# A decayed-attention, top-2 experts and feed-forward kernel on one core: one tile's routing in runs on VectorE, TensorE's fillers in a PSUM bank of their own, changed costs and due times in the scheduler, router constants loaded first

## The chip, the cores and the metric

The kernel runs on one core of one Trainium2 chip. The metric is device time in microseconds (us), the median over timed runs; lower is better. Five engines work side by side, each through its own list of instructions in order: TensorE (PE; its weight loads are shown as PEld), VectorE (DVE), ScalarE (ACT), GpSimd (POOL) and SyncE (SP, which only issues DMA transfers). An instruction waits on semaphores that other engines or transfers raise. SBUF is the on-chip memory that all of them read and write; PSUM is the one that TensorE writes to, in banks of 128 x 512 float32.

## The reference

Three layers follow each other, for 3072 tokens of 384 numbers.

```python
# 1. attention: 4 batches, 8 heads, 768 steps, 48 numbers per head
for t in range(S):
    state = alpha[:, :, t, :, None] * state + np.einsum('bhd,bhe->bhde', k[:, :, t], v[:, :, t])
    y[:, :, t] = np.einsum('bhd,bhde->bhe', q[:, :, t], state)
x = y.transpose(0, 2, 1, 3).reshape(B * S, H * D)          # 3072 x 384
# 2. eight experts, two of them for each token
logits = x @ w_gate
noisy = logits + np.log1p(np.exp(x @ w_noise)) * noise
top2 = indices of the two largest of 8;  top2_w = softmax over the two
h = np.maximum(x[mask] @ w1[e], 0.0)                       # 384 -> 1024
out[mask] += top2_w[mask, k, None] * (h @ w2[e])           # 1024 -> 384
# 3. last layer
h = x @ w_in                                               # 384 -> 2048
return np.maximum(0.01 * h, h) @ w_out                     # 2048 -> 384
```

## The kernel before

**Attention.** The 3072 tokens are 24 units of 128 tokens; four units form a tile, so there are six tiles (0 to 5). SyncE loads three tiles per unit: `at` (the decays, 112x517 float32), `kq` (keys and queries, 112x1024) and `nv` (values, 128x512). ScalarE takes a sum of squares of `at` (L959). VectorE then does the same list for each unit: a backward scan `suf` over 512 columns (L965), twice a reciprocal of two columns and a forward scan `wt` over 256 (L973, L974), the scaled keys `kt` (L988) and the scaled queries `qp` (L992). TensorE transposes the keys, multiplies scores `pS`/`pT` (L1013), updates the state `pM` (L1048, L1052) and sums `pY` (L1069, L1076). GpSimd applies the causal masks to the scores (L1022) and the decay to the state (L1039). The last step of a unit on TensorE is `turn_y` (L1098): four matmuls transpose y into the bank `pA` and multiply it by the router's weights, which stand beside the identity in `turn_w`. ScalarE copies the transposed rows out (into a tile named `xg`), VectorE reduces the logits `lg` (L1107).

**Fillers.** Where the scheduler sees a gap on TensorE it puts in matmuls with the identity whose results nobody reads (`keep_busy`, L919). They write into the last 128 columns of the PSUM tile `pC`. The first columns of that same tile are the operands `d1f`, `d1b`, `scb` of the three scans: `pC` is written by L973 and read by L965 and L974.

**Routing of a tile.** When its four logits are there, a chain of some 30 small operations, called links, runs: `gate_top2` (L204 on, mostly 128x32 on VectorE, three on ScalarE) yields noisy logits `g_z`, the maxima `g_m` and the one-hot choices `g_oh`; three more links count the choices (L1145 to L1153); TensorE and ScalarE make positions out of the counts (L1162, into `pA`); and three links (L1174, L1180, L1184) yield `si`, the slot of each row in the buffer `x_s` in DRAM. GpSimd then scatters the tile's rows into their slots by eight indirect DMAs (L1191), two for each unit.

**Experts and last layer.** Each expert's rows lie in `x_s` in groups: the rows of the first four tiles for experts 0 and 1 (`EARLY`, `EARLY_TILES`), which are worked on first, then the other groups. A group's rows are loaded (L526, tile `xg`), three transposed blocks of 128 go through `pA` (L600), ScalarE rounds them to `xh`, and VectorE subtracts, to `xl` (L609). Expert weights come in four blocks per expert, each a `w1s` (128x768) and a `w2s` (128x768), and are split in the same way into a rounded part (ScalarE, L464) and a rest (`split_lo`, L468, on VectorE or GpSimd, whichever the scheduler finds earlier). TensorE then forms each product in three passes (hi x hi, lo x hi, hi x lo): `ph` (L742) and `py` (L781). The last layer takes the sums of each token's two experts and runs through the same loops.

**The order.** A class `Planner` writes all instruction lists before the kernel runs. Every step has an engine (or a choice "vg" of VectorE and GpSimd), an assumed duration, predecessors, rings of buffers that it takes and holds, and a due time, which is the earliest of those of its successors less their durations, and of a time given by hand. The planner steps through an assumed clock: it takes the step that can start first on any engine, and among several ready ones the one due first. The phase of attention is 1, that of the experts 2. The ring `pA` has two buffers (`ps2`, a pool of two PSUM banks); `turn_y`, the positions and the row transpositions take turns in it. Dependencies between transfers and reads are found by the framework; `apart` removes those among scatters and loads that touch different slots, so that a load of first rows waits for the scatters of tiles 0 to 3 and not for later ones.

## Time and profile before

| | |
|---|---|
| median of 3 timed runs | 1096.68 us (1092.26 to 1100.07) |
| the profiled execution | 1087.71 us |
| its span, first to last instruction | 1085.9 us |
| granted TensorE clock, mean | 0.983 of full speed |
| TensorE busy | 1042.8 us (96%) |
| VectorE busy | 593.7 us (55%) |
| ScalarE busy | 388.2 us (36%) |
| GpSimd busy | 278.5 us (26%) |

Busy time is a mean over stages that differ. In the strip of 40 slices of the span (27.1 us each) TensorE shows 6 tenths in the first slice, 8 in the fifth, 5 in the seventh (163 to 190 us), 7 in the last and 9 or more in all others; the granted clock is lowest in the seventh, with 7 tenths. All durations in the rows below come from the one profiled execution, which lies 9.0 us below the median of the timed runs.

### The profile page before, as it was taken

What the parts mean: (1) busy time and instruction counts of PE and PEld (TensorE: products, weight loads), DVE (VectorE), ACT (ScalarE), POOL (GpSimd) and SP (SyncE); (2) the same over time, 40 slices, a digit from 0 to 9 for tenths busy, and PEclk for the clock granted to TensorE, in tenths of its full rate; (3) what the DMA queues carried; (4) which work ended last, traced back from release to release, by engine and by line L of the source; (5) the groups of instructions that cost most, each with busy time, mean ns of one, the idle gap of its engine ahead of it and who ended that gap; (6) DMA issues with size and microseconds to landing.
All of it is one profiled execution on the core that took longest, in us unless ns stands there. A gap on an engine that the chain in (4) does not pass through costs nothing.

```text
span 1085.9 us, 18172 instructions
## 1 busy us (share of the span) xinstructions
PE 1042.8 (96%) x6839; PEld 999.2 (92%) x6839; DVE 593.7 (55%) x1218; ACT 388.2 (36%) x825; POOL 278.5 (26%) x321
## 2 busy tenths in 40 slices
PE   6999895999999999999999999999999999999997
PEld 5887775999999999999999989899999999999997
DVE  5998997223464565646574233455554545454543
ACT  3755644223354544445453222222222222212211
POOL 3466876200032253424351021410110100000000
PEclk9998997999999999999999999999999999999999
DMA  9667746413464565746567344320101100000000
GB/s 232 203 203 242 237 129 222 157 50 103 148 201 141 179 200 164 226 142 207 180 222 241 116 153 139 92 66 9 59 22 45 34 33 16 22 1 23 1 22 26
DMA packets 78917, 133.20 MB, mean 123 GB/s; under 512 B 8514, under 2 KB 56260, under 8 KB 78820
## 3 DMA queue, kind: packets, MB, share of 16 engines
q1 hardware_dynamic: 72292, 111.89, 33.2%
q0 software_dynamic: 6528, 20.06, 5.7%
q8 instruction: 56, 0.92, 0.4%
q14 instruction: 41, 0.34, 0.1%
HBM read 93.38 MB, written 38.54 MB: 121 GB/s over the span
## 4 chain that ended last, share of the span: by engine, by line
PE 87%; DVE 8%; issue 2%; DMA 1%; ACT 1%; another core or an unknown queue 1%; POOL 0%; DVEq 0%; ACTq 0%; POOLq 0%
PE py L781 39%; PE ph L742 39%; PE pA L600 2%; DVE wt L974 1%; PE pS L1013 1%; DVE suf L965 1%; PE pA L1098 1%; PE pY L1069 1%; PE pC L919 1%; PE pY L1076 1%; DVE kt L988 1%; PE pM L1048 1%; DMA xg<-y_d,gidx 1%; DVE g_z L225 0%
## 5 line engine op out<-in xcount | busy, mean ns | idle before, releaser
L766 DVE SCALAR_TENSOR_TENSOR hl<-ph,hh 128x384 fp32r<-128x384 f32 (+1 forms) x128 | 77.4, 606 | 192.3 <-ACT hh L759 186.1
L752 ACT ACTIVATE hc<-ph 128x384 f32<-128x384 f32 x128 | 63.0, 492 | 300.6 <-PE ph L742 283.3
L755 DVE SCALAR_TENSOR_TENSOR hc<-hc 128x384 f32<-128x384 f32 x128 | 71.4, 558 | 178.2 <-ACT hc L752 178.2
L759 ACT ACTIVATE hh<-ph 128x384 fp32r<-128x384 f32 (+1 forms) x128 | 68.0, 532 | 241.7 <-PE ph L742 236.0
L781 PE MATMUL py<-w2hA,hh 128*128 128x384 f32 (+1 forms) x416 | 141.5, 340 | 1.1 <-issue 1.1
L781 PE MATMUL py<-w2hB,hh 128*128 128x384 f32 (+1 forms) x416 | 141.9, 341 | 0.2 <-issue 0.2
L781 PE MATMUL py<-w2lB,hh 128*128 128x384 f32 (+1 forms) x416 | 140.5, 338 | 0.4 <-issue 0.4
L781 PE MATMUL py<-w2hB,hl 128*128 128x384 f32 (+1 forms) x416 | 140.5, 338 | 0.0
L781 PE MATMUL py<-w2hA,hl 128*128 128x384 f32 (+1 forms) x416 | 140.0, 337 | 0.0
L781 PE MATMUL py<-w2lA,hh 128*128 128x384 f32 (+1 forms) x416 | 139.9, 336 | 0.0
L742 PE MATMUL ph<-xh,w1hA 128*128 128x384 f32 (+1 forms) x384 | 136.4, 355 | 1.4 <-ACT hc L752 0.7
L742 PE MATMUL ph<-xl,w1hA 128*128 128x384 f32 (+1 forms) x384 | 134.3, 350 | 1.0 <-issue 1.0
L742 PE MATMUL ph<-xh,w1hB 128*128 128x384 f32 (+1 forms) x384 | 134.1, 349 | 0.4 <-DVE hl L766 0.4
L742 PE MATMUL ph<-xh,w1lA 128*128 128x384 f32 (+1 forms) x384 | 134.1, 349 | 0.0
L742 PE MATMUL ph<-xl,w1hB 128*128 128x384 f32 (+1 forms) x384 | 133.4, 347 | 0.0
L742 PE MATMUL ph<-xh,w1lB 128*128 128x384 f32 (+1 forms) x384 | 133.3, 347 | 0.0
L804 POOL DMA_INDIRECT xg<-y_d,gidx x48 | 46.5, 968 | 279.6 <-PE pA L600 172.7
L781 PEld LDWEIGHTS py<-w2lA,hh 128*128 128x128 f32 (+1 forms) x416 | 77.3, 186 | 2.2 <-issue 1.2
L781 PEld LDWEIGHTS py<-w2lB,hh 128*128 128x128 f32 (+1 forms) x416 | 77.6, 187 | 1.3 <-issue 0.3
L781 PEld LDWEIGHTS py<-w2hB,hh 128*128 128x128 f32 (+1 forms) x416 | 77.5, 186 | 0.8
L769 DVE TENSOR_TENSOR hl<-hc,hh 128x384 fp32r<-128x384 f32 x128 | 71.4, 558 | 12.3 <-DVE hh L761 0.5
L781 PEld LDWEIGHTS py<-w2hB,hl 128*128 128x128 f32 (+1 forms) x416 | 77.6, 187 | 0.5 <-issue 0.5
(160 smaller groups left out, 1877.3 us busy)
## 6 DMA issues: line engine op xcount, KB each, us to landing
w1s<-in_moe_w_dram SPq DMA_DIRECT2D x32, 384.0 KB
w2s<-in_moe_w_dram SPq DMA_DIRECT2D x32, 384.0 KB
kq<-in_kq_l_dram SPq DMA_DIRECT2D x24, 448.0 KB
nv<-in_v_l_dram SPq DMA_DIRECT2D x24, 256.0 KB
w1s<-in_moe_w_in_dram SPq DMA_DIRECT2D x24, 256.0 KB
w2s<-in_moe_w_out_dram SPq DMA_DIRECT2D x16, 384.0 KB
xg<-x_s SPq DMA_DIRECT2D x32, 180.0 KB
y_d<-ys SPq DMA_DIRECT2D x32, 180.0 KB
```

What stands on the lines that cost most here:

```text
L600: nc.tensor.transpose(p[:, d, :n], src[:n, d * 128:(d + 1) * 128], identf[:n, :n])
L742: nc.tensor.matmul(ps[:, :n], a[:, d, fo:fo + 128], x[:, d, :n], start=i == 0, stop=i == len(seq) - 1)
L752: nc.scalar.activation(hc[:, :n], ps[:, :n], AF.Copy)
L755: nc.vector.scalar_tensor_tensor(hc[:, :n], hc[:, :n], 0.01, hc[:, :n], op0=OP.mult, op1=OP.max)
L759: nc.scalar.activation(hh[:, :n], ps[:, :n], AF.Relu)
L766: nc.vector.scalar_tensor_tensor(hl[:, :n], ps[:, :n], 0.0, hh[:, :n].bitcast(FT), op0=OP.max, op1=OP.subtract)
L769: nc.vector.tensor_sub(hl[:, :n], HT[si, "hc"][:, :n], hh[:, :n].bitcast(FT))
L781: nc.tensor.matmul(py[:n, :], h[:, o:o + n], w[:, f % 2, :], start=(f == 0 and i == 0), stop=(f == nf - 1 and i == 2))
L804: nc.gpsimd.indirect_dma_start(out=yg, out_offset=None, in_=y_d[0:rows, :], in_offset=bass.IndirectOffsetOnAxis(ap=gidx[:, c, kk:kk + 1], ...
L919: nc.tensor.matmul(warm, identf, identf, start=True, stop=True)
L965: nc.vector.tensor_tensor_scan(rev(d["suf"][:, :]), rev(d["at"][:, 1:NW + 1]), rev(d1b), 0.0, OP.mult, OP.add)
L974: nc.vector.tensor_tensor_scan(d["wt"][:, i * hc:(i + 1) * hc], d["at"][:, i * hc:(i + 1) * hc], scb[:, 0:hc], 0.0, OP.mult, OP.add)
```

## The change

What it does, part by part:

- *Fillers.* The filler matmuls write a PSUM tile `pW` of their own instead of the end of `pC`. To have a bank for it, the pool `ps2` goes from two buffers of `pA` to one. In the experts' phase a second bank `pB`, in a pool that exists there, takes turns with `pA` for the transpositions of rows.
- *Loads of rows.* A load of rows now waits, by a dependency added by hand, for all scatters that stand ahead of it in the program (first rows: all those of tiles 0 to 3); only the first load of each kind carries it.
- *Runs.* For tile 3 (`FUSED`) successive links on one engine become one step of up to ten (`RUN`), and the three links to `si` one step of three. The link `um` of the gate is moved ahead of ScalarE's `ln` for all tiles, so that the run of VectorE isn't broken there.
- *Due times.* The transposition and split of the first expert's rows get the due time `TURN` = 0, the constants' load `LCD` = 0. The check of limits and the filling of free slots (`violations`) wait for the start of a later group. One more `xg` buffer (11 to 12).
- *Splits.* In phase 1 `split_lo` may run on VectorE only; in phase 2 still on either.
- *The planner.* It now keeps a time `port`: steps marked `port=True` (weight splits, links on VectorE, `kt`, `qp`, and GpSimd's masks, decays and totals) are not planned beside each other on VectorE and GpSimd. Engines start at given times instead of 0, and several assumed durations change.

```diff
-    NEAR, FAR, SLACK, RATE, LAND = 0.1, 0.25, 0.8, 0.26, 2.0
-    GAP, FILL, COLD, AHEAD, MARGIN = 0.45, 0.24, 0.45, 0.3, 3.0
+    NEAR, FAR, SLACK, RATE, LAND = 0.1, 0.25, 0.8, 0.25, 2.0
+    GAP, FILL, COLD, AHEAD, MARGIN = 0.45, 0.24, 0.42, 0.3, 3.0
...
+        for st in self.steps:
+            st.due = min(st.due, st.own)
...
-                    t0 = max(t, self.free[e])
+                    t0 = max(t, self.free[e], self.port if st.port and e in "vg" else 0.0)
...
+            if st.port and e in "vg":
+                self.port = t0 + dur
...
-    ps2 = fctx.enter_context(tc.tile_pool(name="psum2", bufs=2, space=PSUM))
+    ps2 = fctx.enter_context(tc.tile_pool(name="psum2", bufs=1, space=PSUM))
...
+        first_rows = g == 0 and e < EARLY
+        if first_rows not in awaited:
+            for other in scattered:
+                if not (first_rows and other in late):
+                    tc.add_manual_dep(ins.ins, other.ins.name, SYNC, reason="the rows of every choice are in their slots")
+            awaited.append(first_rows)
...
-        p = XP[key, j] = ps2.tile([128, KD, 128], FT, name="pA")
+        pool, nm = (ps2, "pA") if bank_of[key, j] == "pA" else (pools["P"], "pB")
+        p = XP[key, j] = pool.tile([128, KD, 128], FT, name=nm, bufs=1)
...
-                AUX[i].append([hi, add("vg", dict(v=0.87, g=1.8), lambda en, m=m: split_lo(i, m, en), [hi],
-                                       use=[(fe, R[nm]), (WO[i], R["W"])], phase=phase)])
+                AUX[i].append([hi, add("vg" if phase == 2 else "v", dict(v=0.87, g=1.8) if phase == 2 else 0.87, lambda en="v", m=m: split_lo(i, m, en), [hi],
+                                       use=[(fe, R[nm]), (WO[i], R["W"])], phase=phase, port=True)])
...
-        scb, warm = bank[:PP, 0:HB * C + C], bank[:, HB * C + C:]
+        scb, warm = bank[:PP, 0:HB * C + C], psum.tile([128, 512], FT, name="pW", bufs=1)
...
-                nc.tensor.matmul(warm, identf, identf, start=True, stop=True)
+                nc.tensor.matmul(warm[:, 0:128], identf, identf, start=True, stop=True)
...
+            def links(ops):
+                runs = []
+                for eng, fn in ops:
+                    if gr in FUSED and runs and runs[-1][0] == eng and len(runs[-1][1]) < RUN:
+                        runs[-1][1].append(fn)
+                    else:
+                        runs.append((eng, [fn]))
+                for eng, fns in runs:
+                    dur = small if len(fns) == 1 else (small + 0.08) * len(fns)
+                    link(eng, dur, lambda fns=fns: [fn() for fn in fns], n=len(fns))
...
-        rc = add("g", 6.0, route_consts, due=at_unit(2))
-        ld = add("s", 0.14, load_consts, lat=2.5, due=at_unit(1))
-        consts_in = add("g", 0.2, lambda: nc.gpsimd.tensor_copy(turn_w[:, :, P2:], wgn), [ld, rc], due=at_unit(2))
+        rc = add("g", 3.05, route_consts, due=0.0)
+        ld = add("s", 0.8, load_consts, size=0.13, due=LCD)
+        consts_in = add("g", 0.33, lambda: nc.gpsimd.tensor_copy(turn_w[:, :, P2:], wgn), [ld, rc], due=at_unit(2))
```

The planner's numbers don't say where an instruction ends up; the instruction lists do. In the changed kernel's file the lines lie 11 to 34 further down.

**VectorE's start.** Ahead of the first unit's second forward scan and the second unit's first steps, VectorE's list before was this; what a row waits for stands in brackets (PE is TensorE's semaphore, DMAHW those of transfers):

```order
L974 SCALAR_TENSOR_TENSOR wt<-at,pC 112x256 [waits DVE_49]
L965 SCALAR_TENSOR_TENSOR suf<-at,pC 112x512 [waits DMAHW2_49,PE_49]
L992 TENSOR_TENSOR qp<-kq,wt 112x512 [waits DVE_49]
L973 RECIPROCAL pC<-suf 112x2 [waits DVE_49]
L974 SCALAR_TENSOR_TENSOR wt<-at,pC 112x256 [waits DVE_49]
L988 TENSOR_TENSOR kt<-kq,suf 112x512 [waits DMAHW3_49]
L973 RECIPROCAL pC<-suf 112x2 [waits DVE_49,PE_49]
```

In the changed kernel the same place reads:

```order
L995 SCALAR_TENSOR_TENSOR wt<-at,pC 112x256 [waits DVE_49]
L986 SCALAR_TENSOR_TENSOR suf<-at,pC 112x512 [waits DMAHW2_49]
L1013 TENSOR_TENSOR qp<-kq,wt 112x512 [waits DVE_49]
L994 RECIPROCAL pC<-suf 112x2 [waits DVE_49]
L995 SCALAR_TENSOR_TENSOR wt<-at,pC 112x256 [waits DVE_49]
L1009 TENSOR_TENSOR kt<-kq,suf 112x512 [waits DMAHW5_49]
L994 RECIPROCAL pC<-suf 112x2 [waits DVE_49]
```

The order of the operations is the same; the two waits on TensorE, at `suf` and at the last reciprocal, are gone.

**Tile 3's gate.** This is where the gate of the fourth tile stands on VectorE before, link by link between the attention operations of two units (`g_` names are links):

```order
L221 TENSOR_TENSOR g_um<-g_um,g_ru 128x32
L988 TENSOR_TENSOR kt<-kq,suf 112x512
L225 TENSOR_TENSOR g_z<-g_ln,g_um 128x32
L992 TENSOR_TENSOR qp<-kq,wt 112x512
L229 TENSOR_TENSOR g_z<-g_z,noise_sb 128x32
L965 SCALAR_TENSOR_TENSOR suf<-at,pC 112x512
L233 TENSOR_TENSOR g_z<-g_z,lg 128x32
L973 RECIPROCAL pC<-suf 112x2
L974 SCALAR_TENSOR_TENSOR wt<-at,pC 112x256
L241 TENSOR_REDUCE g_m<-g_z 128x4
L973 RECIPROCAL pC<-suf 112x2
L974 SCALAR_TENSOR_TENSOR wt<-at,pC 112x256
```

And now:

```order
L232 TENSOR_TENSOR g_um<-g_um,g_ru 128x32
L236 TENSOR_TENSOR g_z<-g_ln,g_um 128x32
L240 TENSOR_TENSOR g_z<-g_z,noise_sb 128x32
L244 TENSOR_TENSOR g_z<-g_z,lg 128x32
L252 TENSOR_REDUCE g_m<-g_z 128x4
L257 TENSOR_TENSOR g_ca<-g_z,g_m 128x32
L261 TENSOR_TENSOR g_ca<-g_ca,desc 128x32
L265 TENSOR_REDUCE g_cm<-g_ca 128x4
L269 TENSOR_TENSOR g_oh<-g_ca,g_cm 128x32
L276 SCALAR_TENSOR_TENSOR g_z<-g_oh,g_z 128x32
L289 TENSOR_TENSOR g_wd<-g_m 128x4
L252 TENSOR_REDUCE g_m<-g_z 128x4
```

Ten links stand in a row (the first ten rows), then one, then a second run of eight, the first row of which is the last here; it ends with the three counts (`ot`, `run`, `acc`). Some attention operations that stood between the links now stand ahead of the run or behind it. The slots `si` of this tile come behind 44 forward scans of VectorE's list, where they came behind 46.

**The handover.** Here the first expert's rows are split on VectorE (`xl`). Before, its list there was this:

```order
L468 TENSOR_TENSOR w1lB<-w1s,w1hB 128x768 [waits DMAHW3_49,DMAHW5_49,DMAHW0_49,Activation_49]
L221 TENSOR_TENSOR g_um<-g_um,g_ru 128x32 [waits DVE_49,Activation_49]
L225 TENSOR_TENSOR g_z<-g_ln,g_um 128x32 [waits DVE_49]
L229 TENSOR_TENSOR g_z<-g_z,noise_sb 128x32 [waits DVE_49]
L233 TENSOR_TENSOR g_z<-g_z,lg 128x32 [waits DVE_49]
L241 TENSOR_REDUCE g_m<-g_z 128x4 [waits DVE_49]
L246 TENSOR_TENSOR g_ca<-g_z,g_m 128x32 [waits DVE_49]
L250 TENSOR_TENSOR g_ca<-g_ca,desc 128x32 [waits DVE_49]
L254 TENSOR_REDUCE g_cm<-g_ca 128x4 [waits DVE_49]
L609 TENSOR_TENSOR xl<-pA,xh 128x3x128 [waits Activation_49]
```

Now it is this:

```order
L479 TENSOR_TENSOR w1lA<-w1s,w1hA 128x768 [waits DMAHW1_49,Activation_49]
L303 TENSOR_TENSOR wts<-g_wd,g_ws 128x4
L479 TENSOR_TENSOR w2lA<-w2s,w2hA 128x768 [waits DMAHW2_49,Activation_49]
L627 TENSOR_TENSOR xl<-pA,xh 128x3x128 [waits Activation_49] x2
L479 TENSOR_TENSOR w2lA<-w2s,w2hA 128x768 [waits DMAHW6_49,Activation_49]
L627 TENSOR_TENSOR xl<-pA,xh 128x3x128 [waits Activation_49]
L1128 TENSOR_REDUCE lg<-pA 128x16 [waits Activation_49]
L216 TENSOR_SCALAR g_u<-g_ex 128x32 [waits Activation_49]
L220 SCALAR_TENSOR_TENSOR g_um<-g_u,g_ex 128x32 [waits DVE_49]
L479 TENSOR_TENSOR w1lB<-w1s,w1hB 128x768 [waits DMAHW7_49,DMAHW5_49,Activation_49]
```

The third `xl` stood behind seven links of the sixth tile's gate; now it stands behind the last of eight weight splits, all of which are VectorE's, and the sixth tile's gate follows. On TensorE the same place was, before (`L919` are fillers, `L1098` the transposition of a unit's y, `L600` that of gathered rows; `L1162` belongs to the sixth tile's positions):

```order
L1076 MATMUL pY<-qp,sp 48x128 x7
L919 MATMUL pC<-identf 128x128 x4
L1098 MATMUL pA<-turn_w,xt 128x112 [waits Activation_49]
L1098 MATMUL pA<-turn_w,xt 128x112 x3
L600 MATMUL pA<-identf,xg 128x128 [waits DMAHW0_49,DVE_49]
L600 MATMUL pA<-identf,xg 128x128 x2
L600 MATMUL pA<-identf,xg 128x128 [waits DMAHW1_49,DVE_49]
L600 MATMUL pA<-identf,xg 128x128 x2
L600 MATMUL pA<-identf,xg 128x128 [waits DMAHW2_49,DVE_49]
L600 MATMUL pA<-identf,xg 128x128 x2
L1162 LDWEIGHTS tri
L1162 MATMUL pA<-ot,tri 128x32 [waits DVE_49]
```

And it is now (`L940` fillers, `L618` gathered rows, `L1119` the transposition of y, `L763` the first expert's matmuls):

```order
L618 MATMUL pA<-identf,xg 128x128 [waits DMAHW3_49,DVE_49]
L618 MATMUL pA<-identf,xg 128x128 x2
L940 MATMUL pW<-identf 128x128 x7
L618 MATMUL pA<-identf,xg 128x128 [waits DMAHW4_49,DVE_49]
L618 MATMUL pA<-identf,xg 128x128 x2
L940 MATMUL pW<-identf 128x128 x7
L618 MATMUL pA<-identf,xg 128x128 [waits DMAHW5_49,DVE_49]
L618 MATMUL pA<-identf,xg 128x128 x2
L940 MATMUL pW<-identf 128x128 x7
L1119 MATMUL pA<-turn_w,xt 128x112 [waits DVE_49]
L1119 MATMUL pA<-turn_w,xt 128x112 x3
L763 MATMUL ph<-xh,w1hA 128x384 [waits PE_49,Activation_49]
```

Three times seven fillers stand between the transpositions, and the sixth tile's positions no longer stand ahead of the first expert's matmul. On SyncE's queue the last `w2s` block of expert 0 stands directly behind the three loads of first rows. On GpSimd's list the five splits that stood between masks and scatters in phase 1 are gone; seven splits now stand ahead of the sixth tile's eight scatters. In all the order has 70 filler matmuls where it had 35 (the profile counts two records for each); 25 of the 35 stood at TensorE's start, the others in twos and fours later. About 29 steps take `pA` in phase 1.

## Rows read from the trace of the kernel before

**Rows 1.** Table of stages, whole span. Columns: length, busy us (instructions) per engine, granted clock, DMA share, GB/s.

```profile
0.00:18.38 18.38, 8.62 (x42) 8.22 (x42) 7.03 (x13) 3.89 (x8) 3.38 (x22) 0.92 0.92 223
18.38:166.53 148.15, 137.04 (x1752) 116.60 (x1751) 133.96 (x332) 87.64 (x210) 97.47 (x133) 0.95 0.68 209
166.53:178.56 12.03, 2.17 (x12) 1.38 (x13) 10.53 (x26) 5.83 (x13) 8.28 (x7) 0.60 0.82 265
178.56:182.54 3.98, 3.98 (x14) 3.98 (x13) 2.76 (x14) 0.72 (x2) 1.75 (x2) 0.50 0.14 50
182.54:1078.10 895.56, 889.89 (x5019) 868.32 (x5019) 439.43 (x835) 288.68 (x591) 167.61 (x159) 1.00 0.33 105
```

**Rows 2.** Who waited for the fillers of L919: us, times.

```profile
  DVE suf L965: 5.0, 1
  DVE pC L973: 4.5, 3
```

**Rows 3.** Timeline, 144 to 176: start, us, instruction, idle before and its releaser.

```profile
144.34 0.17 DVE L1184 SCALAR_TENSOR_TENSOR si<-pk,g_cm 128x8 uint32<-128x8 f32 x1 [0.18 <-DVE pk L1180]
...
159.38 1.52 POOL L1191 DMA_INDIRECT x_s<-xg,si  x1 [0.18 <-issue]
...
161.50 0.41 SPq L526 DMA_DIRECT2D xg<-x_s  x1
...
164.14 0.32 SPq L526 DMA_DIRECT2D xg<-x_s  x1
...
166.53 1.02 PE L600 MATMUL pA<-identf,xg 128*128 128x128 f32 x6 [1.51 <-DMA xg<-x_s]
...
174.78 0.55 DVE L609 TENSOR_TENSOR xl<-pA,xh 128x384 fp32r<-128x384 f32 x1
...
175.38 0.90 PE L600 MATMUL pA<-identf,xg 128*128 128x128 f32 x3 [7.83 <-DVE xl L609]
```

**Rows 4.** Timeline of VectorE and GpSimd, 169 to 179.

```profile
169.27 4.25 DVE L225 TENSOR_TENSOR g_z<-g_ln,g_um 128x32 f32<-128x32 f32 x1
...
178.37 0.94 DVE L468 TENSOR_TENSOR w1lB<-w1s,w1hB 128x768 fp32r<-128x768 f32 x1
...
169.89 1.82 POOL L468 TENSOR_TENSOR w1lB<-w1s,w1hB 128x768 fp32r<-128x768 f32 x1
```

**Rows 5.** Timeline of ScalarE and GpSimd, 0 to 19.

```profile
7.93 0.64 ACT L959 ACTIVATE scr<-at 112x517 bf16<-112x517 f32 x1 [3.52 <-DMA at<-in_al_l_dram]
...
18.38 0.24 POOL L1231 COPY turn_w<-wgn 128x64 f32<-128x64 f32 x1 [13.12 <-DMA wgn<-in_wgp_l_dram]
```

**Rows 6.** Timeline of VectorE, the fifth unit's backward scan.

```profile
29.58 1.21 DVE L965 TENSOR_TENSOR_SCAN suf<-at,pC 112x512 f32<-112x512 f32 x1
```

**Rows 7.** VectorE by line and form, 0 to 180: busy us, mean ns, idle before.

```profile
L974 DVE TENSOR_TENSOR_SCAN wt<-at,pC 112x256 f32<-112x256 f32 x48 | 32.9, 686 | 1.7
L973 DVE RECIPROCAL pC<-suf 112x2 f32<-112x2 f32 x48 | 8.1, 168 | 4.8 <-PE pC L919 4.5
```

**Rows 8.** GpSimd by line and form, 0 to 166.6: its weight splits.

```profile
L468 POOL TENSOR_TENSOR w1lA<-w1s,w1hA 128x768 fp32r<-128x768 f32 x3 | 5.4, 1813 | 0.0
L468 POOL TENSOR_TENSOR w2lA<-w2s,w2hA 128x768 fp32r<-128x768 f32 x2 | 3.6, 1813 | 0.0
```

**Rows 9.** Timeline of VectorE, 47 to 50.5: links between attention operations, and in a row.

```profile
47.73 0.18 DVE L246 TENSOR_TENSOR g_ca<-g_z,g_m 128x32 f32<-128x32 f32 x1
47.83 0.68 DVE L992 TENSOR_TENSOR qp<-kq,wt 112x512 f32<-112x512 f32 x1
...
50.12 0.19 DVE L246 TENSOR_TENSOR g_ca<-g_z,g_m 128x32 f32<-128x32 f32 x1
50.34 0.19 DVE L250 TENSOR_TENSOR g_ca<-g_ca,desc 128x32 f32<-128x32 f32 x1
```

**Rows 10.** Timeline of TensorE and VectorE, a `turn_y` and the last of its logits.

```profile
160.56 1.15 PE L1098 MATMUL pA<-turn_w,xt 128*128 128x112 f32 x8
...
162.54 0.33 DVE L1107 TENSOR_REDUCE lg<-pA 128x16 f32<-128x64 f32 x1
```

82 lines of the change are left out of this document (47 added, 35 removed).

## Prediction

> **What bounds the kernel now.** First the page: TensorE is busy 96% of the span, but that is a mean over unlike stages, so I cut the span with the table of stages [rows 1]. From 182.54 on TensorE works 889.89 us of 895.56 at a granted clock of 1.00: experts and last layer leave 5.7 us idle, and the change takes no matmul from them. What can move lies ahead. To 18.38 TensorE is busy 8.62 us. From 18.38 to 166.53 (attention with routing) VectorE is busy 133.96 us of 148.15 and TensorE 137.04, so either may end last. From 166.53 to 178.56 TensorE does 2.17 us of 12.03: the handover to the first expert. [...]
>
> Second, who waits in the first stage. VectorE stood 5.0 and 4.5 us for the filler matmuls of L919 [rows 2], because fillers write into the tile that holds the scans' zero operand: a wait on a neighbour in the bank, not on data.
>
> Third, the handover [rows 3]. The first gathered rows arrive for their transposition at 166.53, but the third transposition starts at 175.38, having stood 7.83 us for `xl` on VectorE. That `xl` ran at 174.78 behind the sixth tile's gate, one operation of which took 4.25 us [rows 4].
>
> **The change, step by step.** I follow one instant, S: the slots `si` of tile 3, at 144.34 [rows 3]. The scatters of the first expert's rows wait for it.
>
> *Fillers in their own bank.* The excerpt of VectorE's start shows two waits on TensorE gone. At most 9.5 us come back [rows 2]. What is late next is the loads. A unit brings 226, 448 and 256 KB by the shapes of its three tiles. The fifth unit's `at` is the fifteenth transfer of the queue; with the constants (32 and 96 KB) now ahead of it, 4.1 MB must pass, at 223 GB/s [rows 1] by 18.3 us. The second `at`, 0.90 MB by its place and so due at 4.0, was waited for until 7.93 [rows 5], 3.9 late, since transfers share the engines. So the fifth lands between 18.3 and 22.2; I take 21. VectorE's own work for the four units before it, 4.3 us each (1.21, four times about 0.69 and two reciprocals of 0.17 [rows 6, 7]), ends near 21 too. The scan on it started at 29.58 [rows 6]: gain 8.0, bounds 7.4 and 9.5.
>
> *Constants first.* GpSimd's copy of the router's weights ran at 18.38 after 13.12 us of waiting [rows 5]; nothing behind it was due before the first score, at that same time [rows 1]. Loaded first, they are there before the score that now comes sooner. 0.13 MB at 223 GB/s delays the second unit's keys by 0.6 us, which the 21 above contains. Taken at nothing; uncovered it would cost those 0.6.
>
> *Splits off GpSimd in the first phase, and the scheduler's port rule.* Before the handover GpSimd ran five weight splits of 1.81 us, 9.0 in sum [rows 8]. What they can do to VectorE is seen at 169.27: 4.25 us for a 128x32 product, with a GpSimd split from 169.89 [rows 4]; one of that shape otherwise has 0.19 [rows 9]. Bounds: none of the 9.0 comes back, or all. I take 4.0, a little under the middle, since scans stood beside some splits. The eight splits cost VectorE 0.94 us each [rows 4], but the new order has all of them behind S; they come in below.
>
> *Tile 3 in runs.* Between two attention operations a link costs VectorE 0.10 (start to start, 47.73 to 47.83); behind another link it costs 0.22 (50.12 to 50.34) [rows 9]. The excerpt has 18 links in runs: 18 x 0.12 = 2.2 us more, bounds 0 and 2.2. The run ends sooner in the program, but the slots do not follow it: 44 forward scans stand ahead of `si` where 46 stood. Two with their reciprocals are 1.7 us [rows 7]: -1.7.
>
> [...]
>
> *One bank `pA` in attention instead of two.* A transposition of y now waits until the bank is read: from the end of the one at 160.56 (1.15 us) to the end of its logits at 162.87 [rows 10], 1.2 us. Bounds: 0, or 1.2 for each of some 29 users (35). I take 1.0 in all, near zero, as every two users in the new order have at least 0.6 us of other matmuls or fillers between them.
>
> Sum to S: -8.0 - 4.0 + 2.2 - 1.7 + 1.0 = -10.5, so S falls at 133.8.
>
> *From S to the first expert.* The eight scatters keep masks between them: the last one started at 159.38 and took 1.52, so it ended 16.6 us after S. The third load of rows, which waited for it, was issued at 164.14, 3.2 later [rows 3]. Now all loads wait for all eight scatters. They are three of 0.20 MB, and on SyncE's queue the fetch of the last `w2s` of expert 0 (0.39 MB) stands right behind them: 0.98 MB at the 265 GB/s of the handover [rows 1] is 3.7 us, and one load alone took 5.0 from issue to use (161.50 to 166.53 [rows 3]): 6.0 for the four. Then, by the excerpt of the handover, ScalarE's rounding of that block (taken like VectorE's) and VectorE's split, 0.94 each [rows 4], the third `xl`, 0.55 [rows 3], and the last transposition of y, 1.15 [rows 10], with 0.7 for the steps between engines: 10.3. So the first expert's matmul starts at S + 16.6 + 3.2 + 10.3 = S + 30.1 = 163.9, where it stood at S + 34.2: 14.7 us earlier than 178.56, bounds 10 and 20 by the terms above. VectorE's own list in between (8 splits, 35 links, 3 `xl`, a unit and a half of attention: about 25 us) is covered by those 30; without that cover it would be the end.
>
> *Clock.* 3.98 us at 0.50 [rows 1] cost 2.0 us. The new order puts 21 fillers between the last transpositions. Bounds 0 and 2.0; I take 1.0.
>
> *After that* TensorE's list is the same work; its 5.7 us of idle time may shift: zero, bounds +3 and -3.
>
> Sum: -15.7. The profiled execution took 1087.71 us, so 1072.0 after. It lies 9.0 below the median of the timed runs, 1096.68; I take the saving off the median: 1081.0.
>
> **The rivals.**
>
> *The gain to S is eaten.* From 18.38 on TensorE is as busy as VectorE [rows 1], and its fillers double from 35 to 70 in the order. The 25 ahead of the first three waits held VectorE 9.5 us [rows 2], 0.38 each at the lower clock, half at the higher: 7 us for 35 more if they stand where TensorE has work. Then S gains 3.5, the shorter handover 4.1: 7.6 us, 1089. For it: 137.04 us of work in 148.15. Against: fillers are placed where the planner saw a gap. Chance 0.16.
>
> *The port follows the splits.* On VectorE a split reads two SBUF operands, as the stalled operation of rows 4 does, so a GpSimd mask may hold it off or be held off by it. Then the 4.0 us do not come back, and of the eight splits some three delay the scatters by 0.94: 15.7 - 4.0 - 2.8 = 8.9 us, 1088. [...] Chance 0.11.
>
> *The single bank decides, and it is slower.* If TensorE stood 1.2 us at each of 29 users of `pA`, 35 us would go, 34 more than I take: 1081 + 34 = 1115. From 14 exposed users on the gain is gone. For it: no second buffer. Against: the order spreads them. Chance 0.05.
>
> *More than forecast.* All of 9.5 and 9.0 come back, runs and bank cost nothing, the clock stays up: 1.5 + 5.0 + 2.2 + 1.0 + 1.0 make 26 us, 1070. Chance 0.06.
>
> **How the numbers follow.** My forecast has 0.62, within 1081 by about 7 either way. About 1% (11 us) is what a measurement of this kernel can tell from no change, so faster begins below 1085.7: 0.58 of the forecast's chance and the better case's 0.06, 0.64. The cases of 1088 and 1089 and the forecast's weak edge are within 1%: 0.31. Slower: 0.05. The range goes from 1071 to 1092; it leaves out the slow case, most of the better one and the edges of the rest.
>
> **What would show it.** Right, step by step: no wait of VectorE for fillers in the first 25 us and the fifth unit's scan near 21; `si` of tile 3 near 134; no GpSimd split ahead of the handover; the third `xl` right behind a split, and the first expert's matmul near 164 at a clock near 1.00; the experts' stage within 3 us of 895.56. Wrong: a first expert matmul after 170; VectorE operations beside masks at several times their usual length; TensorE standing at transpositions of y for the logits; or a gap of TensorE between the first and second round of the two early experts, where the sixth tile's scatters now follow seven GpSimd splits.

## The result and the profile after

| | before | after |
|---|---|---|
| median of the timed runs | 1094.47 us (1090.24 to 1100.07, 4 runs) | 1080.07 us (1077.67 to 1082.60, 4 runs) |
| ratio, with its 95% interval | | 0.987 (0.9826 to 0.9913) |
| span of the profiled execution | 1085.9 us | 1078.8 us |
| slots `si` of tile 3 | 144.34 us | 130.42 us |
| first expert's matmul | 178.56 us | 164.46 us |
| from there to the end of the span | 907.3 us | 914.3 us |

The kernel became 14.4 us faster by the medians; 15.7 were forecast, taken off the 1096.68 us of the first three timed runs: 1081.0 us, within 1071 to 1092. The stages of the changed kernel's trace, cut at the same events as those of before [rows 1] (columns as there):

```profile
0.00:18.38 18.38, 16.94 (x172) 15.67 (x174) 14.49 (x27) 9.24 (x20) 7.93 (x32) 1.00 0.94 264
18.38:154.35 135.97, 126.58 (x1646) 107.66 (x1643) 125.07 (x317) 80.31 (x197) 79.43 (x116) 0.99 0.69 207
154.35:164.46 10.11, 6.97 (x61) 6.59 (x60) 3.78 (x7) 2.48 (x5) 5.89 (x6) 1.00 0.97 335
164.46:168.20 3.74, 3.74 (x16) 3.74 (x15) 1.57 (x5) 2.33 (x7) 0.00 (x0) 0.54 0.45 170
168.20:1070.95 902.75, 892.88 (x5022) 869.99 (x5022) 449.34 (x862) 292.02 (x597) 182.44 (x169) 0.99 0.34 106
```

In the first 18.38 us VectorE now works 14.49 us where it worked 7.03. The first gathered rows arrive at 154.35 (166.53 before). The last stage is 7.2 us longer than its 895.56 of before: TensorE's idle time in it went from 5.7 to 9.9 and its busy time from 889.9 to 892.9.

VectorE's start and GpSimd's copy of the router's weights, in the timeline (start, us, instruction, idle before and its releaser), to be set beside [rows 5, 6]:

```profile
6.61 0.24 POOL L1265 COPY turn_w<-wgn 128x64 f32<-128x64 f32 x1 [1.12 <-DMA wgn<-in_wgp_l_dram]
...
20.54 1.20 DVE L986 TENSOR_TENSOR_SCAN suf<-at,pC 112x512 f32<-112x512 f32 x1
```

The fifth unit's scan starts at 20.54 instead of 29.58, and nobody waits for the fillers any more. The way from the slots to the first expert, to be set beside [rows 3]:

```profile
130.42 0.17 DVE L1215 SCALAR_TENSOR_TENSOR si<-pk,g_cm 128x8 uint32<-128x8 f32 x1 [0.55 <-DVE pk L1211]
...
144.98 1.66 POOL L1225 DMA_INDIRECT x_s<-xg,si  x1 [0.30 <-issue]
...
151.06 1.39 SPq L537 DMA_DIRECT2D xg<-x_s  x3
...
154.35 0.49 PE L618 MATMUL pA<-identf,xg 128*128 128x128 f32 x3
...
158.43 0.55 PE L618 MATMUL pA<-identf,xg 128*128 128x128 f32 x3
...
162.41 0.49 ACT L622 ACTIVATE xh<-pA 128x384 fp32r<-128x384 f32 x1 [3.70 <-issue]
...
164.46 0.49 PE L763 MATMUL ph<-xh,w1hA 128*128 128x384 f32 x1
```

From the slots to the first expert's matmul it takes 34.0 us, as before (34.2). The whole gain of 14.1 us at that matmul was already there at the slots (13.9). ScalarE began the third `xh` at 162.41, 3.4 us after its transposition had ended, with no releaser that the trace knows.

To see where VectorE's 13.9 us went I summed its instructions up to the slots, in four parts. Idle is the sum of the idle times in brackets. Stretch is each instruction's duration less the shortest of the same line and shape. Work is these shortest durations times their counts. The rest is what is left to the slots' start; it is negative because the durations of neighbouring instructions overlap (a link of 0.18 us from 47.73, the next operation from 47.83, [rows 9]), and it grows toward zero where they overlap less. The second traces are those of the first experiment below.

| us up to `si` of tile 3 | idle | stretch | work | rest | sum |
|---|---|---|---|---|---|
| before | 17.7 | 18.5 | 119.4 | -11.4 | 144.3 |
| after | 8.3 | 12.9 | 117.3 | -8.0 | 130.4 |
| difference | -9.4 | -5.6 | -2.1 | +3.4 | -13.9 |
| before, second trace | 12.9 | 25.0 | 118.3 | -12.0 | 144.2 |
| after, second trace | 11.6 | 12.1 | 117.0 | -8.2 | 132.5 |
| difference | -1.3 | -12.9 | -1.3 | +3.8 | -11.7 |

(Sums are of unrounded parts.) The two pairs agree in the sum but not in the parts. In the second pair nearly the whole gain is stretch, and almost no idle time is saved: the 9.4 us of waits for fillers are gone there too, but 7.8 us of waits for logits, which the second trace of before doesn't have, stand in their place (the rows are in the experiment on the bank's two prices).

### The profile page after: what moved, and what is told of

It is laid out like the page before. It is cut to its first block, busy times and chain, and to the rows that moved or that the text cites. A ratio compares the mean times of both kernels' runs of the same rounds, so it can differ in the third digit from the quotient of the medians.

```text
span 1078.8 us, 18282 instructions
## 1 busy us (share of the span) xinstructions
PE 1048.2 (97%) x6909; PEld 1004.4 (93%) x6909; DVE 594.3 (55%) x1215; ACT 387.9 (36%) x826; POOL 275.7 (26%) x323
## 4 chain that ended last, share of the span: by engine, by line
PE 85%; DVE 8%; issue 3%; DMA 1%; ACT 1%; another core or an unknown queue 1%; POOL 1%; DVEq 0%; POOLq 0%; ACTq 0%
PE py L802 40%; PE ph L763 39%; DVE suf L986 2%; DVE wt L995 2%; PE pB L618 1%; PE pA L618 1%; PE pA L1119 1%; DVE qp L1013 1%; PE pY L1090 1%; PE pY L1097 1%; DVE kt L1009 1%; DMA xg<-y_d,gidx 1%; PE pS L1034 1%; DMA w1s<-in_moe_w_dram 0%
## 5 line engine op out<-in xcount | busy, mean ns | idle before, releaser
L763 PE MATMUL ph<-xh,w1hA 128*128 128x384 f32 (+1 forms) x384 | 136.4, 355 | 2.4 <-issue 2.4
L763 PE MATMUL ph<-xh,w1lA 128*128 128x384 f32 (+1 forms) x384 | 134.1, 349 | 1.1 <-issue 1.1
L763 PE MATMUL ph<-xh,w1hB 128*128 128x384 f32 (+1 forms) x384 | 134.3, 350 | 0.9 <-DVE hl L787 0.9
L763 PE MATMUL ph<-xl,w1hA 128*128 128x384 f32 (+1 forms) x384 | 134.5, 350 | 0.0
L763 PE MATMUL ph<-xl,w1hB 128*128 128x384 f32 (+1 forms) x384 | 133.7, 348 | 0.0
L763 PE MATMUL ph<-xh,w1lB 128*128 128x384 f32 (+1 forms) x384 | 133.6, 348 | 0.0
L763 PEld LDWEIGHTS ph<-xh,w1hA 128*128 128x128 f32 x384 | 72.8, 190 | 6.1 <-issue 4.2
```

What stands on the lines that cost most here:

```text
L763: nc.tensor.matmul(ps[:, :n], a[:, d, fo:fo + 128], x[:, d, :n], start=i == 0, stop=i == len(seq) - 1)
```

## The experiments

The runs form three groups beside the two kernels of the result, each from one chip: the first four kernels (the kernel before ran there in 1080.09 us), the second four (1093.96) and the third four (1093.41). Times are therefore given against the kernel before of the same group. Where a kernel of the second or third group is set against the changed one, that is taken at 0.987 of before; the interval of that ratio alone is about 5 us to either side. In the first group the changed kernel has one execution.

### Both kernels again

No edit. 

> The kernel before, unchanged, for a second trace of it. In the first trace its TensorE stood 5.9 us in all behind the first expert's matmul, and that execution (1087.71 us) was the shortest of all of before; in the changed kernel's trace TensorE stands 9.7 us there, and most of the 14.1 us won up to the first expert's matmul is lost again between 190 and 215 us and near 680. Theory A (those stalls differ from execution to execution, and the first trace of before was a lucky one): a second trace shows the first expert's matmul near 178.6 again but 3 to 8 us more lost behind it, and 1090 us or more. Theory B (the change itself brings the stalls): the second trace looks like the first, within 2 us at each place, and the time lies near 1088.

> The changed kernel, unchanged, for a second trace of it. Theory A (stalls differ from execution to execution): the slots of tile 3 at 130 to 131 and the first expert's matmul at 164 to 165 again, but what is lost between 190 and 215 us differs by some us from the 7.8 us of the first trace. Theory B (the stalls belong to the order): the same losses at the same places, within 1 us.

Measured: one execution each, 1080.22 and 1067.63 us. The slots came at 144.18 and 132.53, the first expert's matmul at 176.88 and 163.94. Behind that matmul 901.6 and 901.9 us passed. The table of stages from that matmul on, of the second traces of before and of the changed kernel (columns as in [rows 1]; nearly the same number of matmuls):

```profile
176.88:1070.90 894.02, 892.17 (x5034) 872.09 (x5034) 442.10 (x848) 289.47 (x593) 169.78 (x160) 1.00 0.34 106
```

```profile
163.94:1058.00 894.06, 889.85 (x5036) 868.64 (x5035) 450.28 (x866) 294.66 (x603) 184.36 (x170) 1.00 0.35 109
```

So behind the first expert the two kernels take the same time, to 0.3 us, and the 12.9 us won ahead of it stay to the end (12.7 by the spans). Of the 14 traces in this study, the four of this group have 901 to 902 us there and nine of the ten others 909 to 916; the first trace of before, with 907.3, is the short one among them. Theory B falls: the longer stage behind the first expert doesn't belong to the changed order, whose second trace doesn't have it. Theory A is right in that these stalls differ from trace to trace (TensorE lost 5.1 us from 190 to 215 in the first trace of the changed kernel, 1.0 in the second), but its own forecast missed: the second trace of before lost less and not 3 to 8 us more there, and came at 1080 us and not at 1090 or above. That the first trace of before lacked stalls of its timed runs (1087.7 against 1090.2 to 1100.1), so that the difference of the two first spans, 7.1, is too small, fits all this but isn't shown, since those runs have no trace. Taking the saving off the median rather than off the profile came out right.

### The fillers back in the scans' bank

```diff
-        scb, warm = bank[:PP, 0:HB * C + C], psum.tile([128, 512], FT, name="pW", bufs=1)
+        scb, warm = bank[:PP, 0:HB * C + C], bank[:, HB * C + C:]
```

> The changed kernel, with the fillers back in the last columns of the bank that holds the scans' operands; the order of all instructions stays as it is. If the waits of VectorE for fillers are the price, as the forecast has it (8.0 us, bounds 7.4 and 9.5): VectorE waits 8 to 10 us for L940 in the first 25 us, the fifth unit's backward scan goes from 20.5 to about 29, tile 3's slots from 130.4 to about 139, and the time rises by 8 to 11 us, 1088 to 1091. Rival (the loads decide at the start, and the bank is worth little): the scan stays below 24 and the time within 3 us of the changed kernel's.

Measured: 1079.83 us (10 runs), ratio to before 1.000 (0.9981 to 1.0018): the whole gain gone. Who waited for the fillers in this kernel (us, times), and the fifth unit's scan in its timeline:

```profile
  DVE pC L994: 6.8, 3
...
  DVE suf L986: 5.4, 1
```

```profile
30.32 1.21 DVE L986 TENSOR_TENSOR_SCAN suf<-at,pC 112x512 f32<-112x512 f32 x1
```

These four waits are 12.2 us. A fifth belongs to them, though the trace puts it down to a later semaphore: 4.7 us of VectorE at a reciprocal, which ended with a row of 20 filler records.

```profile
130.71 0.17 DVE L994 RECIPROCAL pC<-suf 112x2 f32<-112x2 f32 x1 [4.73 <-PE pA L1194]
...
126.04 4.64 PE L940 MATMUL pC<-identf 128*128 128x128 f32 x20 [5.32 <-DVE wt L995]
```

Against these 16.9 us VectorE waits 4.0 us less for logits (3.8 against 7.8). Its slots fall at 144.97 against 132.53, and the time is 12.2 us above the changed kernel's single execution on that chip. The order of all instructions is the same, so this is the price of the neighbour in the bank alone: forecast 8.0, bounds 7.4 to 9.5; 9.9 at the fifth unit's scan, and 2.6 more up to the slots. The rival, that the loads decide at the start, falls: the scan did not stay below 24.

### One part alone: the bank's two prices

Both kernels are the one before with this edit, and with `pA` and `pB` in turn for the experts' rows; the second leaves out its last two lines (fillers stay in `pC`). Their instructions stand in the same order as each other's, but not in that of the kernel before: with one bank to give out the planner lays the lists anew, VectorE's from 44 us on, and 297 of its instructions instead of 288 come ahead of the slots.

```diff
-    ps2 = fctx.enter_context(tc.tile_pool(name="psum2", bufs=2, space=PSUM))
+    ps2 = fctx.enter_context(tc.tile_pool(name="psum2", bufs=1, space=PSUM))
...
-            scr=1, pA=2, xg=XGB,
+            scr=1, pA=1, pB=1, xg=XGB,
...
-        scb, warm = bank[:PP, 0:HB * C + C], bank[:, HB * C + C:]
+        scb, warm = bank[:PP, 0:HB * C + C], psum.tile([128, 512], FT, name="pW", bufs=1)
```

> The kernel before with one part of the change alone: fillers in a bank of their own, pA with one buffer, pA and pB in turn for the transpositions of rows in the experts' phase; the planner's rings follow, all else of the planner is as before. Theory (the fillers' waits carry nearly all of the gain, as putting them back into pC cost 12.2 us): VectorE loses its 9.4 us of waiting for fillers, the slots of tile 3 fall at 136 to 138 instead of 144.2, and the time is 6 to 9 us below before. Rival (the single bank gives it back): VectorE waits 4 to 8 us for logits behind pA instead, and the time is within 3 us of before.

> The same as own_bank_before, with the same order of instructions, but with the fillers still in the last columns of pC: the price of the single pA bank by itself, against the kernel before. The forecast put that price at 1.0 us (bounds 0 and 35). The changed kernel's traces have VectorE waiting 3.2 to 7.9 us for transpositions of y and the copies that free the bank. If the forecast's step is right: within 2 us of before. If the bank costs what those waits say: 3 to 8 us above before, with the waits in rows of lg. By the difference to own_bank_before the fillers' share is 8 to 12 us in either case.

Measured: with both, 1098.90 us, ratio 1.0044 (1.0028 to 1.0060); with the single bank only, 1107.95 us, 1.0124 (1.0102 to 1.0145). The logits on VectorE up to the slots, by line (count, busy us, mean ns, idle before and who ended it): in the second trace of before, in the single-bank kernel and in the changed kernel's second trace.

```profile
L1107 DVE TENSOR_REDUCE lg<-pA 128x16 f32<-128x64 f32 x18 | 3.8, 210 | 0.0
```

```profile
L1109 DVE TENSOR_REDUCE lg<-pA 128x16 f32<-128x64 f32 x20 | 4.3, 213 | 6.7 <-ACT xg L1104 4.4 <-issue 2.3
```

```profile
L1128 DVE TENSOR_REDUCE lg<-pA 128x16 f32<-128x64 f32 x19 | 4.1, 215 | 7.8 <-PE pA L1119 4.8 <-ACT xg L1123 2.9
```

With the single bank the slots moved from 144.2 to 152.2, and the kernel lost 14.0 us in all; the fillers' own bank, in the same order, gave 9.0 of them back. Of the 8.0 us at the slots 6.7 are waits for logits; VectorE's work ahead of them also grew by 2.8 us, against 1.1 less stretch. So this is the price of the bank together with the order that the planner makes of it; the bank alone in the order of before was not run. The forecast's 1.0 us is too small in either order, as the changed kernel's two traces have 3.9 and 7.8 us of these waits. It looked at TensorE, where a transposition waits for the bank; the price appears one engine further, where VectorE reaches logits that are not there yet, because ScalarE's copy or the transposition waited for the unit before.

With both parts the slots came at 142.27 and not at 136 to 138, and the kernel is 4.9 us slower than before: the theory, that the fillers' waits carry nearly all of the gain, falls. The rival, that the single bank gives it back, is right in kind but had the size wrong (3.3 us of waits for logits where it had 4 to 8, and more than 3 us lost).

### Without runs

```diff
-FUSED = ((3,),)
+FUSED = ()
```

> The changed kernel without runs: tile 3's links are planned one by one as those of the other tiles. In its order all 48 forward scans stand ahead of tile 3's slots, where the changed kernel has 44. The forecast had the runs cost 2.2 us in themselves, and two scans less ahead of the slots give 1.7. By its prices four scans with their reciprocals more are 3.4 us later, and 18 links in gaps instead of runs 2.2 earlier: slots 1 to 2 us later, the time within 3 us of the changed kernel's. Rival (the runs are what brings the slots forward, since each link alone waits behind whole attention operations and beside masks): slots 6 to 12 us later, and the time 5 to 12 us above the changed kernel's.

Measured: 1097.81 us, ratio 1.0026 (1.0007 to 1.0044), slower than before, and 18 us above the changed kernel. The slots:

```profile
137.26 0.14 DVE L1215 SCALAR_TENSOR_TENSOR si<-pk,g_cm 128x8 uint32<-128x8 f32 x1
```

By the four parts: idle 6.8, stretch 17.9, work 123.0, rest -10.5. Against the changed kernel's first trace the runs save 5.0 us of stretch and 5.7 us of work ahead of the slots (four scans with their reciprocals and the products beside them), and cost 2.5 in lost overlap (forecast: 2.2) and 1.5 of idle time. The two lists differ in more than the links, so the 2.5 are not the links' alone. The slots come 6.8 us later without runs (4.7 against the second trace), the first matmul 12.0 (176.41). Of the 5.1 us by which the way between them is longer, 3.3 are the eighth scatter, which ends 19.6 us behind the slots instead of 16.2, between masks that come late too; then ScalarE stands 6.7 us beside scatters (last section), which is not the runs' doing. The rival holds in its direction; the 18 us are above its 5 to 12, and how much of them are such stalls isn't known.

### Five splits more on GpSimd

```diff
                     nc.gpsimd.tensor_mul(d["sp"], prev["S"], tots[:, u, :, None].to_broadcast([PP, HP, D]))
+                    decays.append(u)
+                    if len(decays) in (11, 13, 14, 15, 16):
+                        kv = d["kq"].rearrange("p a h c -> p (a h c)")
+                        nc.gpsimd.tensor_sub(work.tile([PP, 768], FT, name="idle", bufs=1), kv[:, 0:768], kv[:, 256:1024])
```

> The changed kernel, with five extra subtractions of 112x768 on GpSimd behind five decays, between 86 and 124 us, where the kernel before had five weight splits of that size; their result is used by nobody, and no other instruction moves. The forecast gave 4.0 us for taking such splits away (bounds 0 and 9.0). If GpSimd's splits hold VectorE off: VectorE's operations beside them are stretched by 4 to 6 us in sum, tile 3's slots come 4 to 6 us later (134.5 to 136.5), and the time rises by as much. Rival (the masks hold VectorE off just as well, and a split more changes only which operation waits): slots within 1.5 us of 130.4 and no change of time. A second rival (GpSimd's own list becomes late, 9 us more of it): masks and scatters late by up to 9 us, with TensorE waiting for masks.

Measured: 1077.77 us, 10.1 above the changed kernel's execution on that chip; slots at 142.10, 9.6 later. Stretch 16.1 against 12.1: 4.0 us, as in the forecast, so the first rival (the masks hold VectorE off just as well) falls. One of the operations, in VectorE's and GpSimd's timelines of this kernel:

```profile
113.02 3.59 DVE L257 TENSOR_TENSOR g_ca<-g_z,g_m 128x32 f32<-128x32 f32 x1
```

```profile
113.51 0.54 POOL L1060 TENSOR_TENSOR sp<-S,tots 112x192 f32<-112x192 f32 x1
113.98 1.83 POOL L1064 TENSOR_TENSOR idle<-kq 112x768 f32<-112x768 f32 x1
```

The other 5.7 are idle time, 5.3 of it at logits: the extra operations read `kq` and so hold its buffers longer, and ScalarE waited 5.6 us for an `at` behind it. That part is the experiment's own doing. Only the stretch speaks for the splits; by the table above it fell by 5.6 and 12.9 in the changed kernel, of which the runs share.

### Without the due time for the first rows

```diff
-TURN = 0.0
+TURN = 1e9
```

> The changed kernel without the due time for the first rows (TURN far off); its order is the same up to the handover, where tile 5's gate again stands ahead of the second and third xl on VectorE, and a transposition of y between the transpositions of rows on TensorE. The forecast gave 4.1 us for the shorter way from the slots to the first expert's matmul (34.2 to 30.1; the traces have 32.7 to 34.2 before and 31.4 to 34.0 after). If the due time is what shortens it: slots as in the changed kernel (130 to 133), the first expert's matmul 4 to 8 us later than its 164, the time 3 to 8 us above the changed kernel's (ratio to before about 0.991 to 0.995). Rival (scatters, loads and weights set the handover, not the order on VectorE): first matmul within 2 us of 164 and the ratio as the changed kernel's, 0.987.

Measured: 1084.47 us, ratio 0.9919 (0.9889 to 0.9949); slots at 128.79, first matmul at 167.84, 39.1 us behind them. Timeline of VectorE, GpSimd and TensorE at its handover:

```profile
160.39 5.44 DVE L257 TENSOR_TENSOR g_ca<-g_z,g_m 128x32 f32<-128x32 f32 x1
160.43 3.59 POOL L479 TENSOR_TENSOR w1lB<-w1s,w1hB 128x768 fp32r<-128x768 f32 x2
163.95 1.82 POOL L479 TENSOR_TENSOR w2lB<-w2s,w2hB 128x768 fp32r<-128x768 f32 x1
165.75 0.54 DVE L627 TENSOR_TENSOR xl<-pA,xh 128x384 fp32r<-128x384 f32 x1
...
166.35 0.90 PE L618 MATMUL pA<-identf,xg 128*128 128x128 f32 x3 [7.33 <-DVE xl L627]
```

This is the stall of [rows 4] again: a link of tile 5's gate stands 5.44 us beside three splits, and the `xl` behind it is what TensorE waits for. The due time puts `xl` ahead of the gate; it is worth 5 us of the way from slots to expert (39.1 against 34.0), as the theory had it. The first matmul itself came only 3.4 us later (4 to 8 were expected), since the slots came earlier. Up to 157 us the order is the changed kernel's, so three traces of one order have these slots at 128.79, 130.42 and 132.53: between single traces a difference under 4 us there says little. The stall itself does not go away; in the changed kernel the same link takes 1.87 us at 172.67, where no transposition waits for it.

### Without the planner's port time

```diff
-                    t0 = max(t, self.free[e], self.port if st.port and e in "vg" else 0.0)
+                    t0 = max(t, self.free[e], 0.0)
```

> The changed kernel with the planner's port time switched off: VectorE's and GpSimd's marked steps may again be planned beside each other; phase 1 splits stay on VectorE. If the planner's rule spares stretched operations: VectorE's stretch ahead of tile 3's slots goes from 12 us to 17 to 25 (before: 19 to 25), the slots come 4 to 10 us later, and the time rises by 4 to 10 us over the changed kernel's. Rival (the stretch is spared by taking the splits off GpSimd alone; a planned clock that is off by microseconds can't keep two engines apart): stretch within 3 us of 12 and slots within 3 us of 131, whatever the order.

Measured: 1087.55 us, ratio 0.9941 (0.9922 to 0.9960), 8 us above the changed kernel. Stretch 15.0 us up to slots at 135.45. So the rule spares little stretch (15.0 against 12.9), as the rival said, but the slots are 3 to 7 us later than in the three traces of the changed order, against it: two more scans stand ahead of them, and the way behind them takes 40.5 us. What the rule gains here comes mostly by the other order that it leads to; neither theory had that.

### Constants as late as the planner likes

```diff
-LCD = 0.0
+LCD = 1e9
```

> The changed kernel with the router's constants loaded when the planner needs them and not first (own due time taken away). The forecast took that edit at nothing, 0.6 at most: GpSimd's copy into turn_w would wait to about 18 us as it did before, the first transposition of y would come behind it, and no more. If so: the slots within 2 us of 131 and the time within 3 us of the changed kernel's. Rival (the first transposition of y and with it the single bank are late for the whole first tile, or masks queue behind the waiting copy): tile 0's slots 3 us or more later than 50 to 52, and the time 4 us or more above.

Measured: 1084.69 us, ratio 0.9925 (0.9906 to 0.9945). The copy into `turn_w` ran at 16.79, tile 0's slots came at 48.73, tile 3's at 132.86. At the start the edit is worth nothing, as forecast. The 5 us come later: 46 scans ahead of the slots instead of 44, and 35.5 us behind them. That this is the constants' doing and not just another draw of the planner can't be told from it, nor are 5 us clear of the uncertainty of the changed kernel's ratio.

### Without fillers, and with fillers at the start only

```diff
-        scb, warm = bank[:PP, 0:HB * C + C], psum.tile([128, 512], FT, name="pW", bufs=1)
+        scb = bank[:PP, 0:HB * C + C]
+        warm = ps2.tile([128, KD, 128], FT, name="pA")
...
-            for _ in range(n):
+            for _ in range(0 if R["pA"].given else n):
...
-            scr=1, pA=1, pB=1, xg=XGB,
+            scr=1, pA=2, pB=1, xg=XGB,
```

This is the second kernel; the first has no `warm` and no fillers at all. Both give `pA` two buffers, have no `pB`, and stand in the same order.

> The changed kernel without any filler matmul; the bank that they held goes back to pA, which has two buffers in both phases. What the fillers are worth: if TensorE's clock is what they keep up and VectorE sets the end of the first phase, TensorE's granted clock in the first 20 us and at the handover is at the lower level, which costs 1 to 4 us, and the second bank gives back 1 to 4: within 3 us of the changed kernel's time. Rival (the clock decides): the first 25 us grow by 5 us or more, and the time rises by 5 to 12 us. Second rival (fillers only cost, and the bank is worth more): 4 to 8 us below the changed kernel's time.

> The kernel without fillers (no_fillers: time ratio to before 0.984, slots at 136.2, TensorE clock 0.90 in the first phase), in the same order of instructions, with the fillers at TensorE's start only; they write into pA ahead of its first use, so that pA keeps two buffers. Meant to beat both kernels. If the low clock at the start is what a kernel without fillers pays: TensorE's clock near 1.00 in the first 25 us, first transposition of y 1 to 3 us earlier, slots 1 to 3 us earlier than 136.2, and 1 to 3 us below no_fillers. Rival (VectorE and the loads set the start; the clock there is worth nothing): slots and time as in no_fillers within 1 us. Second rival (the clock falls behind the start anyhow and nothing lasts): clock 1.00 to 20 us and 0.9 behind, time as no_fillers.

Measured: without fillers 1076.69 us, ratio 0.984 (0.9786 to 0.9895), not to be told from the changed kernel; with fillers at the start 1071.70 us, ratio 0.9801 (0.9781 to 0.9821), the lowest ratio of all, some 7 us below the changed kernel, though the two never ran on one chip. The first 18.38 us of both, without fillers first (columns as in [rows 1]):

```profile
0.00:18.38 18.38, 10.15 (x96) 8.59 (x98) 14.67 (x27) 8.61 (x18) 6.98 (x30) 1.00 0.94 248
```

```profile
0.00:18.38 18.38, 16.71 (x172) 15.34 (x174) 14.49 (x27) 9.35 (x20) 7.95 (x32) 1.00 0.94 261
```

Their slots come at 136.23 and 133.76, their first matmuls at 168.44 and 165.15. The clock reads 1.00 in both stages and 0.88 in both from 25 to 130, so the expected mechanism, a higher clock at the start, isn't shown. The 2.5 us at the slots are less than traces of one order differ by, and the intervals of the two ratios meet, so that the fillers at the start are worth anything isn't shown either. What is shown is that 0.88, against 0.98 in the changed kernel's first trace (25 to 130) and 0.94 in its second (0 to 132.6), costs nothing to be seen in the time, and that fillers need no bank of their own if they stop before `pA` is used. The second kernel was profiled in the longest of its four runs (1077.13), and up to the first expert's matmul that trace is no earlier than the changed kernel's (164.46 and 163.94): where its 7 us come from stays open.

## Why the prediction was right, step by step

| step | forecast | measured | where |
|---|---|---|---|
| fillers' waits, to S | -8.0 | -9.0 at the fifth unit's scan; 12.4 at S in the new order | after, fillers back |
| splits off GpSimd | -4.0 | 4.0 of stretch for five of them | five splits more |
| runs: lost overlap | +2.2 | +2.5 against the kernel without runs, +3.4 and +3.8 against before | without runs, the four parts |
| fewer scans ahead; less stretch by runs | -1.7; not in the forecast | -5.7; -5.0 | without runs |
| single bank `pA` | +1.0 | 6.7 of waits in a new order of the kernel before, 3.9 and 7.8 in the changed kernel's | one part alone |
| sum to S | -10.5 | -13.9 and -11.7 | two pairs of traces |
| S to the first expert | -4.1 | -0.2 and -1.3 | two pairs of traces |
| clock at the handover | -1.0 | -0.2 and -1.8 (the first 12 matmuls: 4.0 to 3.7 us, 4.0 to 2.2) | two pairs of traces |
| behind it | 0 | +0.3; +7.0 in the first pair | second traces |
| time | -15.7 | -14.4 | medians |

The forecast was right in the sum, in part by luck. The slots came 3.4 and 1.2 us earlier than forecast, the way from there to the first expert was 3.9 and 2.8 us longer, and these misses cancelled. The steps on fillers, splits and lost overlap held within their bounds or near them, and the constants cost the start nothing. (The step on fillers has a slip: 29.58 less 21 is 8.6 and not 8.0; measured are 9.0. That transfers share the engines, as it says of the second `at`, shows in the trace of before: the 16 engines are busy for a share of 1.00 from 5 to 10 us, and the second `at` was used 6.2 us after its issue at 1.75, the first 2.9 after 0.82.) Ahead of the slots two more terms were mis-sized and cancelled. The step "one bank `pA`" took a value near zero since every two users have 0.6 us of other matmuls between them. That argument covers TensorE's own waiting and not VectorE's logits, in an order where ScalarE's copy, VectorE's logits and the next transposition follow in turn. Against that, the step "tile 3 in runs" counted scans ahead of the slots between before and after, and not what the slots would be without runs: with runs VectorE's operations are also stretched less (by 5.0 us), and without them the changed kernel is slower than before.

The step "from S to the first expert" had the parts right where it read them from rows: the last scatter ended 16.2 us after S (forecast 16.6), the loads went out 4.4 later (3.2). Then came 13.4 instead of 10.3, for which ScalarE's 3.4 us late `xh` is enough. In the second trace, where ScalarE does not stand so, the way is 31.4, against the forecast's 30.1. The clock's step goes with the same stand in these two traces. In the first the 21 fillers ended 3.0 us before the last transposition of y, and the first matmuls ran at 0.54, near the 0.50 of before [rows 1]. In the second they ended 0.6 us before it, and the first twelve matmuls ran at 1.00:

```profile
163.94:166.13 2.19, 2.19 (x16) 2.19 (x15) 0.64 (x4) 1.63 (x5) 0.68 (x1) 1.00 1.00 382
```

So there the step gave all that its bound of 2.0 had; but TensorE then stood 1.4 and 0.5 us for the next loads of rows at 168.78 and 169.84, and nothing of it was left behind. Of the signs of being wrong, two came. VectorE operations beside masks do take several times their usual length (1.94 us at 111.76 and 1.95 us at 108.15 in the two traces, for a link of 0.19). And in the first trace there is a gap of TensorE beside the sixth tile's scatters (5.1 us), and the last stage was not within 3 us of 895.56; the second trace has 1.0 us there.

Of the rivals, "the gain to S is eaten" by fillers fell: nobody waits for `pW`, and the kernel without fillers isn't clearly faster. The 0.38 us a filler at the lower clock, and half at the higher, that the rival counted with were 0.44 at a granted clock of 0.55 (14.94 to 18.45) and 0.25 at 1.00 (20.63 to 22.15) in the trace of before; from 7.44 to 12.24 they were 0.44 too, where the table reads 1.00. "The port follows the splits" is half right: 12 to 13 us of stretch stay with no split on GpSimd, but 5.6 and 12.9 us came back, and none of the eight splits on VectorE delayed the scatters. "The single bank decides" was real with a larger price than its chance said: in the order that the planner made for it, the kernel before became 14 us slower. "More than forecast" (1070 us) did not come. That a run has a price at all, where the forecast's lower bound had none, agrees with the first trace of the changed kernel: in tile 3's run the first six links, 0.19 us long but for one, start 0.22 to 0.23 us after each other (109.00 to 110.12), and a `kt` starts 0.11 us after the link ahead of it (107.61 to 107.72).

## What to carry to other kernels

A helper that writes beside an operand, in the same tile, became a wait of the operand's reader here (9.5 us before, 12.2 with the fillers back); but a bank taken for it from a ring of two had a price too (6.7 us of waits for logits), and it showed on the engine that reads the ring's results, not on the one that fills it. Undoing one part at a time cost 5 to 18 us each, some 49 in sum (fillers 12, runs 18, port time 8, due time 5, constants 5; the last two are not clear of the noise), where all edits together gave 14: such parts are priced only in the order that they stand in, and an experiment that keeps the order is worth several that don't. Before the trace of one execution is compared with another, split it at an event that both share, and take two of each: here 13 us ahead of the first expert were the change, and 7 behind it were not, while the parts of those 13 (waits, stretch) differed from pair to pair.
